# Attention and a feed-forward layer on one core: five units whose softmax weights and values are multiplied whole, as float32

## The chip, the core and the metric

The kernel runs on one core of a Trainium2 chip. The core has a matrix engine (PE, with its weight loads shown as PEld), a vector engine (DVE), an activation engine (ACT), a general engine (POOL, called gpsimd in the code) and a queue that starts transfers (SP). Each takes its instructions in a fixed order, and they wait for one another by semaphores. The metric is the device time of one execution in microseconds (us); lower is better.

## The reference

```python
scores = scale * np.matmul(q, k.transpose(0, 1, 3, 2))          # 8 batches, 8 heads, 576 x 64
thresh = np.max(scores, axis=-1, keepdims=True) - tau           # tau = 0.02
scores = np.where(scores >= thresh, scores, -1000000000.0)
scores = scores - np.max(scores, axis=-1, keepdims=True)
attn = np.exp(scores)
attn = attn / (np.sum(attn, axis=-1, keepdims=True) + 1e-09)
x = np.matmul(attn, v)                                          # heads side by side: 4608 x 512
h = x @ w_in                                                    # 512 -> 2048
g = np.maximum(h, 0.0) + np.log1p(np.exp(-np.abs(h)))
return g @ w_out                                                # 2048 -> 512
```

Inputs of the attention are float32. The two weight matrices arrive in eight bytes a number and are brought to float32 on the chip. A score just above or just below the threshold changes a row of weights wholly, so products are kept near float32 precision.

## The kernel before, in words

**Units and tiles.** A unit is one batch and one pair of heads: 32 units, in the code `s`. Each has nine tiles of 128 query rows: four of the first head, four of the second, and one (index `NC` = 4) that holds the last 64 rows of both. `g` counts tiles over all units, 0 to 287. For a tile the kernel makes scores on PE (`scores`, L410), the negated row maximum on DVE (`row_max`, L416), exponentials on ACT (`exps`, L424), and the masked exponentials with their row sum on DVE (`mask`, L429). PE transposes them (`weights_T`, L463; the 64 rest columns of two tiles at once, L460), ACT copies them to SBUF (`weights_hi`), and when a group of tiles is there, `values` multiplies them with the values, L536 to L538. A unit has four groups `g` of 256 or 320 columns.

**Two halves.** Most products are made from halves in a reduced type (float32r). `x` is split into `hi`, its rounded copy, and `lo`, what is missing. For the weights that is a tile `gH` with five column blocks (four main blocks and one block that holds the rest rows' high half above their low half) and a tile `gL` with the low part of the four main blocks. For the values it is `vt`: 64 columns of high part beside 64 columns of low part, made on POOL by `split_v` (L118 and L125). A group then takes nine matmuls: four of `gH` and four of `gL` with `vt`, and one for the rest block. The two halves of the output partitions are added: ACT copies one half to `xp`, DVE adds the other (`values_out`).

**Two ways to the low part.** For the first four units (`s.neg`, tiles under `TG` = 36) DVE is spared: PE transposes the exponentials a second time into a bank `tl` (L511), subtracts the high part there by a product with the negative `gH` and an identity (L513), and ACT copies the result to `gL`. DVE still makes the low half of the rest block (L523). From the fifth unit on, DVE subtracts straight from the score bank (L125).

**Order.** The program is written out tile by tile from a string of steps: `PAT0` for the first 36 tiles, `PAT` after them. Letters stand for the steps: R row maximum of the next tile, M mask, T transposes, e exponentials of the next tile, S scores two tiles ahead, h and l the high and low parts, x the extras (values, the next unit's splits and transposes), w one piece of weight preparation every second tile (`W1` = 2, 32 pieces in all), p a point at which deferred steps come due, f feed-forward matmuls. A scheduler may shift neighbouring instructions. Feed-forward work comes by quota per tile and starts about tile 36; the first chunk of 512 tokens is due from tile 41. After the last tile the rest of it runs alone.

**Buffers.** There are two score banks, two halves of `e_all`, four PSUM banks `g` shared by everything else, three `nat` buffers (k, q, v as loaded), three `vt` buffers and two each of `gH` and `gL`.

**Weight pieces.** A piece is loaded, then ACT takes an absolute value (L185), POOL clamps it (L186), DVE puts its bits together in three instructions (L192, L194, L197) and POOL splits it (L118, L125). Feed-forward copies and subtractions are recorded at these last lines too, so the tile name tells them apart.

Of the kernel before, what the change touches and what calls it, by code (L numbers as in the profile page):

```python
# [58 lines left out]
def tile_kernel(ctx: ExitStack, tc: tile.TileContext, q, k, v, tau, w_in, w_out, out):  # L59
# [207 lines left out]
    for b in range(B):  # L267
        for kind in (("one", "two") if b < NSPLIT else ("all",)):
            for hp in range(NPAIR):
# [15 lines left out]
                s.neg = 9 * NPAIR * b + 9 * hp < TG  # L285
# [20 lines left out]
    def load_v(s):  # L306
        s.vn = apool.tile([P, 10, D], F32, tag="nat", bufs=3, name=f"vn_{s.i}")
# [173 lines left out]
    def copy(s, out_, in_):  # L481
        if s.neg:
            nc.scalar.activation(out_, in_, AF.Copy, scale=-1.0)
        else:
            nc.scalar.copy(out_, in_)  # L485

    def weights_hi(s, t):
        main, rest = s.sp[t]
        for g, c0, s0, n in s.place[t]:
            copy(s, group(s, g)[0][:, 0:NC, c0:c0 + n], main[:, :, s0:s0 + n])  # L490
        both = rests(s, t)
        if len(both) == 2:

# [8 lines left out]
    def weights_lo(s, t):
        main, rest = s.sp.pop(t)
        for g, c0, s0, n in s.place[t]:
            h, l = group(s, g)
            if s.neg:
                if s0 == 0:
                    low = ps_g.tile([P, NC, P], F32, tag="g", name=f"tl_{s.i}_{t}")
                    for c in range(NC):
# [1 line left out]
                        nc.tensor.matmul(low[:, c, :], e_all[:, s.half[t], k0:k0 + P], ident, is_transpose=True,  # L511
                                         start=c == 0, stop=False)
                nc.tensor.matmul(low[:, :, s0:s0 + n], identr, h[:, 0:NC, c0:c0 + n], start=False, stop=s0 + n == P)  # L513
# [5 lines left out]
        for x, rows, up, down in rests(s, t):
            for g, c0, s0, n in s.place[x]:  # L520
                h = group(s, g)[0]
                if s.neg:
                    nc.vector.scalar_tensor_tensor(out=h[down, NC, c0:c0 + n], in0=rest[rows, s0:s0 + n], scalar=-1.0,  # L523
                                                   in1=h[up, NC, c0:c0 + n].bitcast(F32), op0=ALU.mult, op1=ALU.subtract)
                else:
                    lo_of(nc.vector, h[down, NC, c0:c0 + n], rest[rows, s0:s0 + n], h[up, NC, c0:c0 + n])
# [14 lines left out]
    def values_out(s, g, o):  # L541
# [4 lines left out]
        copy(s, xs, o[move, 0:n])  # L546
        if s.neg:
            nc.vector.tensor_tensor(out=xs, in0=xs, in1=o[keep, 0:n], op=ALU.subtract)
        else:
# [431 lines left out]
```

## Time and profile before

| | |
|---|---|
| median of 3 runs | 1475.11 us (1473.59 to 1477.98) |
| profiled execution | 1474.09 us, span 1472.3 us |
| mean granted PE clock | 0.991 |
| PE busy | 1405.8 us (95%) |
| PEld busy | 1192.3 us (81%) |
| DVE busy | 1013.3 us (69%) |
| ACT busy | 872.2 us (59%) |
| POOL busy | 604.7 us (41%) |

Busy time is the union of an engine's instruction spans. Matmuls are pipelined, so the spans of neighbours overlap: a matmul's price in a full queue is the distance from one start to the next, not its own length. The whole-program shares mix stages: about 140 us of attention alone, a long middle in which attention and feed-forward share PE, and a tail of feed-forward alone.

### The profile page before, as it was taken

The numbers are of one execution on the slowest core, as the hardware profiler recorded it, in microseconds if no ns is written. First come the engines' busy times: TensorE is split into PE (matmuls) and PEld (weight loads), VectorE is DVE, ScalarE is ACT, GpSimd is POOL, SyncE is SP. The second block draws the span as 40 slices with busy tenths as digits, with TensorE's granted clock in tenths as the row PEclk, the third lists the DMA queues.
The fourth block names the chain that finished last, engine by engine and source line by source line (L and its number), as shares of the span: only waits on it lengthen the run. The fifth ranks groups of instructions, "written<-read, shape, count | busy, mean of one in ns | idle before, by whom it ended". The sixth has DMA issues, their size and how long they took to land.

```text
span 1472.3 us, 23929 instructions
## 1 busy us (share of the span) xinstructions
PE 1405.8 (95%) x8024; PEld 1192.3 (81%) x8024; DVE 1013.3 (69%) x2251; ACT 872.2 (59%) x1671; POOL 604.7 (41%) x629
## 2 busy tenths in 40 slices
PE   6878789999999999999999999999999999999998
PEld 5767677788888888888888888888888888788886
DVE  6998778877777777777777777777777777411211
ACT  6887577566766576656666666657665665411110
POOL 3767565544333433343334433343334332323221
PEclk9999899999999999999999999999999999999999
DMA  5777565434344554335334534454433533344321
GB/s 149 213 203 199 168 200 161 134 111 135 109 121 117 129 150 121 110 107 153 108 101 116 140 106 117 117 139 142 119 113 107 159 93 82 101 136 128 116 86 43
DMA packets 131210, 189.95 MB, mean 129 GB/s; under 512 B 35312, under 2 KB 86800, under 8 KB 131088
## 3 DMA queue, kind: packets, MB, share of 16 engines
q1 hardware_dynamic: 131088, 188.43, 44.2%
q8 instruction: 64, 1.05, 0.3%
q14 instruction: 58, 0.48, 0.1%
HBM read 140.51 MB, written 27.41 MB: 114 GB/s over the span
## 4 chain that ended last, share of the span: by engine, by line
PE 74%; DVE 8%; ACT 7%; issue 4%; POOL 3%; DMA 3%; SPq 1%; POOLq 0%; DVEq 0%; ACTq 0%
PE s L410 10%; PE h L631 8%; PE h L629 8%; PE h L633 8%; PE o L691 7%; PE o L689 7%; PE o L687 7%; PE s L463 7%; PE pv L536 3%; PE pv L537 3%; DVE negm L416 2%; PE tr L351 2%; DVE e_all L429 2%; POOL g L125 1%; DMA wc_i<-in_moe_w_in_dram 1%
## 5 line engine op out<-in xcount | busy, mean ns | idle before, releaser
L485 ACT CAST gH<-s 128x512 fp32r<-128x512 f32 (+1 forms) x448 | 186.7, 466 | 160.8 <-PE s L463 152.8
L125 POOL TENSOR_TENSOR g<-st,g 128x512 fp32r<-128x512 f32 x144 | 192.8, 1357 | 194.2 <-DVE g L122 182.3
L429 DVE SCALAR_TENSOR_TENSOR e_all<-s,thr,e_all 128x576 f32<-128x576 f32 x288 | 234.3, 815 | 37.8 <-ACT e_all L424 34.8
L416 DVE TENSOR_REDUCE negm<-s 128x1 f32<-128x576 f32 x288 | 217.4, 755 | 41.4 <-PE s L410 33.4
L691 PE MATMUL o<-wo_o,g 128*128 128x512 f32 x576 | 232.6, 404 | 5.3 <-POOL g L125 5.3
L631 PE MATMUL h<-xl,wi 128*128 128x512 f32 x576 | 233.1, 405 | 1.7 <-POOL xl L125 1.7
L687 PE MATMUL o<-wo_o,g 128*128 128x512 f32 x576 | 232.9, 404 | 1.0 <-ACT st L651 0.7
L629 PE MATMUL h<-xh,wi 128*128 128x512 f32 x576 | 230.6, 401 | 1.9 <-ACT st L651 1.4
L633 PE MATMUL h<-xh,wi 128*128 128x512 f32 x576 | 230.4, 400 | 0.0
L689 PE MATMUL o<-wo_o,g 128*128 128x512 f32 x576 | 229.7, 399 | 0.0
L424 ACT ACTIVATE e_all<-s,negm 128x576 f32<-128x576 f32 x288 | 215.8, 750 | 10.3 <-DVE negm L416 6.5
L125 DVE TENSOR_TENSOR gL<-s,gH 128x512 fp32r<-128x512 f32 (+1 forms) x280 | 175.0, 633 | 59.1 <-ACT gH L485 55.8
L410 PE MATMUL s<-kT,qT 128*128 128x288 f32 x1024 | 194.3, 311 | 13.3 <-DVE gH L125 5.9
L410 PEld LDWEIGHTS s<-kT,qT 128*128 128x128 f32 x1024 | 150.5, 192 | 33.9 <-issue 11.4
L122 DVE CAST g<-st 128x512 fp32r<-128x512 f32 x128 | 57.4, 485 | 149.6 <-ACT st L651 149.1
L463 PE MATMUL s<-identr,e_all 128*128 128x128 f32 x1008 | 155.7, 277 | 3.8 <-DVE e_all L429 3.8
L651 ACT ACTIVATE st<-h 128x512 f32<-128x512 f32 x144 | 78.3, 596 | 117.3 <-PE h L633 116.7
L536 PE MATMUL pv<-gH,vt 128*128 128x320 f32 (+1 forms) x512 | 143.9, 301 | 1.4 <-ACT gH L485 1.3
L537 PE MATMUL pv<-gL,vt 128*128 128x320 f32 (+1 forms) x512 | 142.8, 300 | 1.5 <-DVE gL L125 1.4
L691 PEld LDWEIGHTS o<-wo_o,g 128*128 128x128 f32 x576 | 108.7, 189 | 29.6 <-POOL g L125 11.0
L463 PEld LDWEIGHTS s<-identr,e_all 128*128 128x128 f32 x1008 | 116.2, 142 | 19.2 <-DVE e_all L429 10.9
L629 PEld LDWEIGHTS h<-xh,wi 128*128 128x128 f32 x576 | 108.9, 189 | 25.4 <-ACT st L651 1.9
(105 smaller groups left out, 2381.1 us busy)
## 6 DMA issues: line engine op xcount, KB each, us to landing
wi<-wi_d SPq DMA_DIRECT2D x144, 512.0 KB
qT<-qT SPq DMA_DIRECT2D x124, 128.0 KB
R<-r_d SPq DMA_DIRECT2D x64, 144.0 KB
kn<-in_k_dram SPq DMA_DIRECT2D x32, 256.0 KB
qn<-in_q_dram SPq DMA_DIRECT2D x32, 256.0 KB
vn<-in_v_dram SPq DMA_DIRECT2D x32, 256.0 KB
wc_i<-in_moe_w_in_dram SPq DMA_DIRECT2D x16, 512.0 KB
wi_d<-wc_i SPq DMA_DIRECT2D x32, 256.0 KB
```

What stands on the lines that cost most here:

```text
L125: eng.tensor_tensor(out=out_, in0=in_, in1=hi.bitcast(F32), op=ALU.subtract)
L410: nc.tensor.matmul(sp[:, hf, 0:HS], lhs, s.kT[j][:, k0 + hf * HS:k0 + (hf + 1) * HS], start=(m == 0), stop=(m == len(parts) - 1))
L416: nc.vector.reduce_max(negm, s.sp[t][:, :, 0:HS], axis=AX.XY, negate=True)
L424: nc.scalar.activation(e_all[:, s.half[t], :].rearrange("p (h n) -> p h n", h=2), s.sp[t][:, :, 0:HS], AF.Exp, bias=s.m[t][0], scale=1.0)
L429: masked.append(nc.vector.scalar_tensor_tensor(out=e2, in0=s.sp[t][:, :, 0:HS], scalar=s.m.pop(t)[1], in1=e2, op0=ALU.is_ge, op1=ALU.mult, ...
L463: nc.tensor.matmul(main[:, c, :], e[:, c0:c0 + P], ident, is_transpose=True, start=True, stop=True)
L629: nc.tensor.matmul(h, wi[:, 0, cc, :], u.h[cc], start=(cc == 0), stop=False)
L631: nc.tensor.matmul(h, wi[:, 0, cc, :], u.l[cc], start=False, stop=False)
L633: nc.tensor.matmul(h, wi[:, 1, cc, :], u.h[cc], start=False, stop=(cc == NCC - 1))
L687: nc.tensor.matmul(o, gh[:, sl], wo[fc][:, 0, :], start=(i == 0), stop=False)
L689: nc.tensor.matmul(o, gh[:, sl], wo[fc][:, 1, :], start=False, stop=False)
L691: nc.tensor.matmul(o, gl[:, sl], wo[fc][:, 0, :], start=False, stop=(i == QF - 1))
```

## The change

For the first five units (`s.whole`, `NF` = 5: the four pairs of batch 0 and the first pair of batch 1) the weights stay whole float32 in `gH`, `gL` is not made, the values are used as they were loaded, and the product is a plain float32 matmul. `split_v` returns at once for them. The loaded values take a `vt` buffer in place of a `nat` buffer. The output has 64 partitions, and ACT copies it to `xp`; no addition follows. The rest block of a group now holds rest rows in one half and zeros in the other: where one rest tile serves two tiles, two ACT instructions write it with a scale per partition of 1 or 0 (`side`, filled once at the start); in the tile of the last 64 rows ACT copies and POOL writes the zeros. The path with the negative copies is gone altogether, so units 0 to 3 lose L511, L513 and L523, and unit 4 loses its subtractions on DVE.

```diff
+    side = cpool.tile([P, 2], F32, name="side")
+    for i in range(2):
+        for j in range(2):
+            nc.vector.memset(side[i * SR:(i + 1) * SR, j:j + 1], float(i == j))
...
-                s.neg = 9 * NPAIR * b + 9 * hp < TG
+                s.whole = len(units) < NF
...
     def load_v(s):
-        s.vn = apool.tile([P, 10, D], F32, tag="nat", bufs=3, name=f"vn_{s.i}")
+        if s.whole:
+            s.vn = apool.tile([P, 10, D], F32, tag="vt", bufs=3, name=f"vn_{s.i}")
+        else:
+            s.vn = apool.tile([P, 10, D], F32, tag="nat", bufs=3, name=f"vn_{s.i}")
...
     def split_v(s, j):
+        if s.whole:
+            return
...
         for g, c0, s0, n in s.place[t]:
-            copy(s, group(s, g)[0][:, 0:NC, c0:c0 + n], main[:, :, s0:s0 + n])
+            h = group(s, g)[0]
+            h = h.bitcast(F32) if s.whole else h
+            nc.scalar.copy(h[:, 0:NC, c0:c0 + n], main[:, :, s0:s0 + n])
...
+                elif len(both) == 2:
+                    nc.scalar.activation(h.bitcast(F32), rest, AF.Copy, scale=side[:, s.half[x]:s.half[x] + 1])
+                else:
+                    nc.scalar.copy(h[up].bitcast(F32), rest[rows, s0:s0 + n])
+                    nc.gpsimd.memset(h[down].bitcast(F32), 0.0)
 
     def weights_lo(s, t):
         main, rest = s.sp.pop(t)
+        if s.whole:
+            return
...
-                    for c in range(NC):
-                        k0 = s.half[t] * SR + c * P
-                        nc.tensor.matmul(low[:, c, :], e_all[:, s.half[t], k0:k0 + P], ident, is_transpose=True,
-                                         start=c == 0, stop=False)
-                nc.tensor.matmul(low[:, :, s0:s0 + n], identr, h[:, 0:NC, c0:c0 + n], start=False, stop=s0 + n == P)
...
     def values(s, g):
...
+        if s.whole:
+            for c in range(NC + 1):
+                nc.tensor.matmul(o[0:D, 0:n], s.vn[:, 5 * j + c, :], h[:, c, 0:n].bitcast(F32),
+                                 start=(c == 0), stop=(c == NC))
+            defer(1, lambda: nc.scalar.copy(s.xp[j * D:(j + 1) * D, x0:x0 + n], o[0:D, 0:n]))
+            return
```

On PE, the end of unit 0's last group (`pv_3`) and the second tile of unit 1, before. A row gives line, operation, output<-inputs and shape; `tr` and `tm` are the transposed rest and main blocks, `s` a score bank, `tl` the bank for the low part, `rT` the transposed row scales.

```order
L536 MATMUL pv_3_663<-gH_3_556,vt_1_230 128x256
L537 MATMUL pv_3_663<-gL_3_557,vt_1_230 128x256
L538 MATMUL pv_3_663<-gH_3_556,vt_1_230 128x256
L460 MATMUL tr_1_685<-identr,e_all 128x128
L463 MATMUL tm_1_684<-identr,e_all 128x128 x4
L410 MATMUL s_137<-kT_0_377,qT_1_0_427 128x288 x2
L410 MATMUL s_137<-kT_0_377,qT_1_0_428 128x288 x2
L511 MATMUL tl_1_698<-identr,e_all 128x128 x4
L513 MATMUL tl_1_698<-gH_0_651,identr 128x512
L560 MATMUL rT_709<-identr,rs_614 9x128
```

The same place after (the new kernel's own lines: its L538 is the float32 product).

```order
L538 MATMUL pv_3_560<-gH_3_482,vn_183 64x256 x5
L472 MATMUL tr_1_577<-identr,e_all 128x128
L475 MATMUL tm_1_576<-identr,e_all 128x128 x4
L422 MATMUL s_142<-kT_0_339,qT_1_0_379 128x288 x2
L422 MATMUL s_142<-kT_0_339,qT_1_0_380 128x288 x2
L565 MATMUL rT_593<-identr,rs_519 9x128
```

The nine products of the group are five, the tile's second set of transposes and the subtraction are gone, and what stands around them keeps its order.

On DVE, from the end of unit 0 into unit 1's second tile, before: `negm` is a row maximum, `e_all,sums` a mask, `wa_i` a weight piece, `gH` the low half of a rest block, `xp` the addition of the two output halves.

```order
L548 TENSOR_TENSOR xp_327<-xp_327,pv_2_568 64x320
L556 RECIPROCAL rs_614<-rs_614 128x9
L429 SCALAR_TENSOR_TENSOR e_all,sums_551<-s_138,thr_0_585,e_all 128x576
L523 SCALAR_TENSOR_TENSOR gH_3_556<-tr_8_590,gH_3_556 64x128 x2
L416 TENSOR_REDUCE negm_1_636<-s_137 128x1
L194 SCALAR_TENSOR_TENSOR wa_i_3_579<-wc_i_3_578,wa_i_3_579 128x512
L416 TENSOR_REDUCE negm_2_679<-s_138 128x1
L429 SCALAR_TENSOR_TENSOR e_all,sums_551<-s_137,thr_1_637,e_all 128x576
L197 SCALAR_TENSOR_TENSOR wa_i_3_579<-wc_i_3_578,wa_i_3_579 128x512
L548 TENSOR_TENSOR xp_327<-xp_327,pv_3_663 64x256
```

And after.

```order
L561 RECIPROCAL rs_519<-rs_519 128x9
L441 SCALAR_TENSOR_TENSOR e_all,sums_477<-s_143,thr_0_498,e_all 128x576
L428 TENSOR_REDUCE negm_1_541<-s_142 128x1
L201 SCALAR_TENSOR_TENSOR wa_i_3_493<-wc_i_3_492,wa_i_3_493 128x512
L428 TENSOR_REDUCE negm_2_571<-s_143 128x1
L441 SCALAR_TENSOR_TENSOR e_all,sums_477<-s_142,thr_1_542,e_all 128x576
L204 SCALAR_TENSOR_TENSOR wa_i_3_493<-wc_i_3_492,wa_i_3_493 128x512
```

The rest blocks and the additions have left the queue; maxima, masks and weight pieces stand in the same order.

On PE in unit 4, from the scores of the tile with the last 64 rows (`qm`) on, before: `pv_1` is the second group, `h_0` and `h_1` are feed-forward products.

```order
L410 MATMUL s_137<-kT_1_1837,qm 128x288 x4
L351 MATMUL tr_0_1_2162<-identr,q_5_0_2084 128x128 x3
L460 MATMUL s_138<-identr,e_all 128x128
L463 MATMUL s_138<-identr,e_all 128x128 x4
L351 MATMUL tr_0_1_2162<-identr,q_5_0_2084 128x128
L410 MATMUL s_138<-kT_1_1837,qT_4_1_1843 128x288 x2
L410 MATMUL s_138<-kT_1_1837,qT_4_1_1844 128x288 x2
L463 MATMUL s_137<-identr,e_all 128x128 x4
L466 MATMUL s_137<-identr,e_all 64x128
L536 MATMUL pv_1_2209<-gH_1_2030,vt_0_1740 128x320
```

And after.

```order
L472 MATMUL s_143<-identr,e_all 128x128
L475 MATMUL s_143<-identr,e_all 128x128 x4
L363 MATMUL tr_0_1_1749<-identr,q_5_0_1674 128x128 x4
L634 MATMUL h_0_1739<-xh_0_1715,wi_0_1733 128x512
L636 MATMUL h_0_1739<-xl_0_1716,wi_0_1733 128x512
L638 MATMUL h_0_1739<-xh_0_1715,wi_0_1733 128x512
L634 MATMUL h_0_1739<-xh_2_1725,wi_0_1733 128x512
L422 MATMUL s_143<-kT_1_1466,qT_4_1_1472 128x288 x2
L422 MATMUL s_143<-kT_1_1466,qT_4_1_1473 128x288 x2
```

Between the transposes into a score bank and the scores that reuse it there now stand four transposes of the next unit's queries and four feed-forward matmuls, where one such transpose stood.

More of the change, by code (lines that the diff above doesn't have):

```diff
@@ L51 @@
 GV = 1
+NF = 5
 TG = 36
@@ L435, in group @@
             h = apool.tile([P, NC + 1, 320], F32R, tag="gH", name=f"gH_{s.i}_{g}")
-            l = apool.tile([P, NC, 320], F32R, tag="gL", name=f"gL_{s.i}_{g}")
+            l = None if s.whole else apool.tile([P, NC, 320], F32R, tag="gL", name=f"gL_{s.i}_{g}")
             s.grp[g] = (h, l)
@@ L489, in weights_hi @@
         for g, c0, s0, n in s.place[t]:
-            copy(s, group(s, g)[0][:, 0:NC, c0:c0 + n], main[:, :, s0:s0 + n])
+            h = group(s, g)[0]
+            h = h.bitcast(F32) if s.whole else h
+            nc.scalar.copy(h[:, 0:NC, c0:c0 + n], main[:, :, s0:s0 + n])
         both = rests(s, t)
-        if len(both) == 2:
+        if len(both) == 2 and not s.whole:
             (g, c0, _, n), = s.place[both[0][0]]
-            copy(s, group(s, g)[0][:, NC, c0:c0 + 2 * n].rearrange("p (k n) -> p k n", k=2),
-                 rest.unsqueeze(1).to_broadcast([P, 2, n]))
+            nc.scalar.copy(group(s, g)[0][:, NC, c0:c0 + 2 * n].rearrange("p (k n) -> p k n", k=2),
+                           rest.unsqueeze(1).to_broadcast([P, 2, n]))
@@ L497, in weights_hi @@
             return
-        for x, rows, up, _ in both:
+        for x, rows, up, down in both:
             for g, c0, s0, n in s.place[x]:
-                copy(s, group(s, g)[0][up, NC, c0:c0 + n], rest[rows, s0:s0 + n])
+                h = group(s, g)[0][:, NC, c0:c0 + n]
+                if not s.whole:
+                    nc.scalar.copy(h[up], rest[rows, s0:s0 + n])
+                elif len(both) == 2:
[3 more added lines that the diff above has]
+                    nc.gpsimd.memset(h[down].bitcast(F32), 0.0)
@@ L516, in weights_lo @@
-        if s.neg:
-            defer(1, lambda: [copy(s, group(s, g)[1][:, :, c0:c0 + n], low[:, :, s0:s0 + n])
-                              for g, c0, s0, n in s.place[t]])
+            lo_of(nc.vector, l[:, :, c0:c0 + n], main[:, :, s0:s0 + n], h[:, 0:NC, c0:c0 + n])
         for x, rows, up, down in rests(s, t):
@@ L521, in weights_lo @@
                 h = group(s, g)[0]
[L522 to L526, printed above, removed]
+                lo_of(nc.vector, h[down, NC, c0:c0 + n], rest[rows, s0:s0 + n], h[up, NC, c0:c0 + n])
     def values(s, g):
@@ L532, in values @@
         h, l = s.grp[g]
+        o = ps_g.tile([P, 512], F32, tag="g", name=f"pv_{s.i}_{g}")
+        if s.whole:
[4 more added lines that the diff above has]
+            return
         vt = s.vt[j]
-        o = ps_g.tile([P, 512], F32, tag="g", name=f"pv_{s.i}_{g}")
         for c in range(NC):
@@ L545, in values_out @@
         xs = s.xp[keep, x0:x0 + n]
[L546 to L549, printed above, removed]
-            nc.vector.tensor_tensor(out=xs, in0=o[keep, 0:n], in1=xs, op=ALU.add)
+        nc.scalar.copy(xs, o[move, 0:n])
+        nc.vector.tensor_tensor(out=xs, in0=o[keep, 0:n], in1=xs, op=ALU.add)
     def row_scales(s):
```

10 lines of the change are left out of this document (removed).

## The prediction

> **What bounds the kernel now.** I read the busy time by unit first: the stretches are unit 0, units 1 to 3, unit 4 (bounds taken from each unit's first mask on DVE), and one late stretch. The columns are length, then busy us of PE, PEld, DVE, ACT and POOL, the granted PE clock, and the DMA share.
>
> ```profile
> 15.50:44.70 29.20, 24.74 (x172) 22.63 (x172) 22.79 (x49) 23.00 (x55) 14.34 (x20) 1.00 0.56 163
> 44.70:74.50 29.80, 26.14 (x187) 22.24 (x184) 28.31 (x56) 26.05 (x62) 20.76 (x22) 1.00 0.78 215
> 74.50:108.50 34.00, 25.75 (x187) 22.30 (x185) 30.67 (x60) 28.65 (x68) 22.86 (x25) 1.00 0.71 207
> 108.50:140.70 32.20, 27.24 (x182) 24.80 (x182) 29.07 (x57) 23.99 (x57) 21.78 (x26) 0.89 0.68 187
> 140.70:189.60 48.90, 39.41 (x208) 32.15 (x207) 37.58 (x79) 31.70 (x60) 32.19 (x35) 0.86 0.63 189
> ...
> 600.00:1300.00 700.00, 692.31 (x4035) 591.68 (x4034) 509.00 (x1171) 437.33 (x810) 259.27 (x264) 1.00 0.42 120
> ```
>
> Late in the program PE is the bound (692.31 of 700 us). In units 1 to 3 it is not: over their 96.0 us DVE is busy 88.05 us (91.7%), PE 79.13 (82.4%), ACT 78.69. The waits of that stretch (total us, times, longest) say the same: PE's two largest are for the mask on DVE.
>
> ```profile
> PE tm L463 <- DVE e_all L429: 6.8, 4, 2.9
> PE tr L460 <- DVE e_all L429: 6.3, 5, 2.5
> ...
> ACT wa_i L185 <- DMA wc_i<-in_moe_w_in_dram: 2.3, 3, 1.1
> ```
>
> The feed-forward quota is counted per tile. Whatever shortens the first 45 tiles moves everything after them forward, and nothing later hands it back unless the work per tile grows.
>
> **DVE in units 0 to 3.** The groups of DVE instructions in the same 96.0 us show what goes.
>
> ```profile
> L429 DVE SCALAR_TENSOR_TENSOR e_all<-s,thr,e_all 128x576 f32<-128x576 f32 x28 | 22.6, 809 | 1.2 <-ACT e_all L424 1.0
> L416 DVE TENSOR_REDUCE negm<-s 128x1 f32<-128x576 f32 x27 | 20.3, 753 | 1.7 <-PE s L410 1.4
> L523 DVE SCALAR_TENSOR_TENSOR gH<-tr,gH 64x128 fp32r<-64x128 f32 x24 | 6.9, 289 | 0.5
> ...
> L548 DVE TENSOR_TENSOR xp<-xp,pv 64x320 f32<-64x320 f32 x6 | 2.9, 484 | 0.5 <-ACT xp L483 0.4
> L548 DVE TENSOR_TENSOR xp<-xp,pv 64x256 f32<-64x256 f32 x6 | 2.5, 417 | 1.7 <-ACT xp L483 1.7
> ...
> L523 DVE SCALAR_TENSOR_TENSOR gH<-tr,gH 64x64 fp32r<-64x64 f32 x6 | 1.0, 213 | 0.1
> ```
>
> Maxima and masks stay. L523 and L548 leave: 6.9 + 1.0 + 2.9 + 2.5 = 13.3 us in three units, 4.4 a unit. DVE falls from 29.35 to 24.9 us a unit.
>
> **PE in units 0 to 3.** Prices are distances from start to start. The columns are start, length, engine, line.
>
> ```profile
> 25.98 0.28 PE L536 MATMUL pv<-gH,vt 128*128 128x256 f32 x1
> ...
> 27.05 0.27 PE L460 MATMUL tr<-identr,e_all 128*128 128x128 f32 x1
> ...
> 42.67 0.31 PE L537 MATMUL pv<-gL,vt 128*128 128x320 f32 x1
> ...
> 43.26 0.27 PE L460 MATMUL tr<-identr,e_all 128*128 128x128 f32 x1
> ...
> 54.54 0.60 PE L511 MATMUL tl<-identr,e_all 128*128 128x128 f32 x4
> 54.90 0.48 PE L513 MATMUL tl<-gH,identr 128*128 128x512 f32 x1
> 55.21 0.28 PE L536 MATMUL pv<-gH,vt 128*128 128x256 f32 x1
> ```
>
> Nine products of 256 columns take 27.05 - 25.98 = 1.07 us, 0.119 each; four of 320 columns take 0.59 us, 0.1475 each. Two groups of either width cost 2 x 1.07 + 18 x 0.1475 = 4.80 us a unit, and these go. The low part costs 0.36 us for four transposes and 0.31 us for the subtraction: 9 x 0.67 = 6.03 us a unit, which go too.
>
> What comes is 20 plain float32 matmuls a unit, and no row shows one. The lower end is one pass at the reduced type's price: 10 x 0.119 + 10 x 0.1475 = 2.67 us. For the upper end I use what this kernel does itself: a number that the reduced type can't hold is two halves, and the whole product of two such numbers has four terms (the feed-forward part writes three and drops low times low). Four passes at the same rows' price are 10.66 us. I take four: a plain float32 matmul has no reason to drop a term. The weight loads I take as hidden, as today's are: a load lasts 0.188 us (rows below) and the products behind each other still start 0.119 us apart.
>
> [...]
>
> PE a unit is then 10.66 - 4.80 - 6.03 = -0.2 us: 26.4 becomes 26.2. PE gains nothing; its work changes kind.
>
> **ACT, POOL, buffers.**
>
> ```profile
> L483 ACT ACTIVATE gL<-tl 128x512 fp32r<-128x512 f32 x24 | 14.4, 600 | 5.3 <-PE tl L513 5.2
> ...
> L483 ACT ACTIVATE gH<-tr 128x256 fp32r<-128x256 f32 x12 | 4.6, 386 | 0.0
> ...
> L483 ACT ACTIVATE gL<-tl 128x256 fp32r<-128x256 f32 x6 | 2.0, 378 | 0.4 <-PE tl L513 0.3
> ...
> L383 ACT ACTIVATE qm<-tr,qscale 128x64 fp32r<-128x64 f32 x6 | 1.6, 327 | 0.0
> ```
>
> ACT loses (14.4 + 2.0) / 3 = 5.5 us a unit of `gL` copies. Four rest copies of 0.386 become eight with a scale per partition; between 0.327 (L383, half as wide) and 0.386 (twice as wide), say 0.35: +1.3 us. Net -4.2 us, 26.2 to 22.0 a unit. POOL loses the split of the values and gets two small memsets a unit. They stand behind the weight pieces in POOL's order, and the products of two groups wait for them:
>
> ```profile
> POOL wa_i L186 <- ACT wa_i L185: 14.2, 8, 4.0
> ```
>
> That clamp has waited up to 4.0 us. The group's products are written a tile (3.5 us) after the memset, so I take nothing, up to 0.5 us a memset. The memsets of `side` stand at the start, where DVE waits for the first loads. The values' loads keep their number and place on SP; only their buffer changes, to one free since three units before. Nothing for both.
>
> **The pace of units 0 to 3.** The longest engine is now PE with 26.2 us a unit. I give it the share that DVE, the longest today, reaches: 26.2 / 0.917 = 28.6 us against 32.0, -3.4 a unit, -10.2 for three. In unit 0 PE is already the longest: (24.74 - 0.2) / 0.917 = 26.8 against 29.2, -2.4. Together -12.6 us.
>
> **Unit 4.** Here nothing is saved on PE: +10.66 - 4.80 = +5.9 us, while feed-forward matmuls fill its queue. DVE loses its subtractions:
>
> ```profile
> L125 DVE TENSOR_TENSOR gL<-s,gH 128x512 fp32r<-128x512 f32 x8 | 5.5, 683 | 5.6 <-ACT gH L485 5.6
> ...
> L125 DVE TENSOR_TENSOR gH<-s,gH 64x128 fp32r<-64x128 f32 x8 | 2.3, 288 | 0.2
> ...
> PE s L410 <- DVE gH L125: 3.5, 1, 3.5
> ...
> PE pv L537 <- DVE gL L125: 0.8, 1, 0.8
> ...
> 158.23 1.30 PE L410 MATMUL s<-kT,qT 128*128 128x288 f32 x4 [3.53 <-DVE gH L125]
> ...
> 161.49 0.63 PE L629 MATMUL h<-xh,wi 128*128 128x512 f32 x1
> 161.92 0.63 PE L631 MATMUL h<-xl,wi 128*128 128x512 f32 x1
> ...
> 166.09 0.40 PE L633 MATMUL h<-xh,wi 128*128 128x512 f32 x1
> 166.32 0.39 PE L629 MATMUL h<-xh,wi 128*128 128x512 f32 x1
> ```
>
> Scores wait for the bank until DVE's last subtraction has read it: 3.5 us once. That wait goes with its cause, and so does the 0.8. Behind the long gap PE runs slowly: the same matmul starts every 0.43 us at 161.5 and every 0.23 us at 166. Some 5 us run so, of which 5 x (1 - 0.23/0.43) = 2.3 come back. Unit 4: +5.9 - 4.3 - 2.3 = -0.7 us.
>
> **The sum** is -12.6 - 0.7 = -13.3 us: span 1472.3 to 1459.0, this execution 1474.09 to 1460.8. The median shown is 1.0 above this execution, so **1462 us**.
>
> **Rivals.** *DVE stays the bound and PE fits under it.* For it: DVE holds the longest waits today. Units 1 to 3 go to 24.9 / 0.917 = 27.2 us, -4.8 each; with unit 0 and 4 as above -17.5: 1458. Against it: PE has more work than DVE.
>
> *The weight pieces take the cover's place.* A piece is loaded a fixed number of steps, about one tile, ahead of its ACT instruction, and ACT has waited 2.3 us for such loads. Tiles that are 3.4 / 9 = 0.38 us shorter give each of the 18 pieces in 36 tiles that much less lead: up to 6.8 us back, in ACT's queue ahead of the exponentials. Net -6.5: 1469. Against it: only three such waits in 27 tiles.
>
> *Slower: the float32 loads stand in the open.* A load today:
>
> ```profile
> L536 PEld LDWEIGHTS pv<-gH,vt x48: 187/188/333, 47.2 to 138.6; 128*128 128x128 f32 x48
> ```
>
> With 64 columns, half of 0.188 us, before each of 80 passes: +7.5 us a unit. PE has 33.7 us, at 0.917 36.8 a unit: +4.8 in three, (24.5 + 7.5) / 0.917 = 34.9 in unit 0, +5.7, and 7.5 - 0.7 in unit 4: +27: 1502. It turns slower once PE passes 32.0 x 0.917 = 29.3 us a unit, 0.04 us a pass. Against it: every load of the trace hides behind the product before it. Any dearer pass than assumed acts at this place.
>
> *Float32 at one pass*, so that the products aren't what the change says: 2.67 us a unit, DVE bound, unit 4 at -2.1 - 4.3 - 2.3 = -8.7: -25.5, 1450. For it: four float32 transposes (L511) cost only 0.09 us each. Against it: a transpose multiplies with ones and zeros.
>
> **How the numbers follow.** Forecast 0.48, DVE bound 0.15, weight pieces 0.18, slower 0.13, one pass 0.05; 0.01 for no effect. The range 1451 to 1475 leaves out the slower case and the one pass. A difference under 0.3% (4.4 us) can't be told from no change. The forecast, the DVE case and the one pass are faster, the weight pieces in three of four, so faster 0.79, within 0.3% 0.08, slower 0.13.
>
> **What would show it.** Right: each float32 product of 320 columns takes about 0.59 us start to start, of 256 about 0.48; a unit of batch 0 takes 28 to 29 us; DVE is under 90% busy there and PE over it; the 3.5 us wait in unit 4 is gone; from 190 us on, all is as before and 13 us earlier. Wrong: products over 0.75 us (five passes); longer waits of ACT's L185 for loads; PE waiting for `gH` behind a POOL memset; or a later stage that takes longer than now.

## The result, and the profile after

| | before | after |
|---|---|---|
| median, same chip | 1474.35 us (1472.26 to 1477.98, 4 runs) | 1458.26 us (1457.67 to 1461.06, 4 runs) |
| profiled execution: span | 1472.3 us | 1456.1 us |
| mean granted PE clock | 0.991 | 0.996 |
| PE / DVE / ACT / POOL busy | 1405.8 / 1013.3 / 872.2 / 604.7 us | 1398.7 / 983.5 / 854.7 / 588.5 us |

The ratio is 0.9893 [0.9875, 0.9911]: 16.1 us less by the medians, 16.2 by the spans. The forecast was 1462 us and 13.3 us less. The size was about right; the place was not.

The next rows give the kernel after by stage: unit 0, units 1 to 3, unit 4. The columns are those of the prediction's first fence: length, then busy us of PE, PEld, DVE, ACT and POOL, the granted PE clock, the DMA share. Units begin at their first mask on DVE.

```profile
14.99:44.70 29.71, 24.05 (x130) 18.33 (x130) 19.65 (x38) 19.88 (x49) 10.62 (x16) 1.00 0.64 189
44.70:136.85 92.15, 75.17 (x423) 52.46 (x423) 71.43 (x129) 65.91 (x168) 57.59 (x70) 0.94 0.72 203
136.85:176.07 39.22, 36.19 (x187) 24.18 (x188) 26.52 (x53) 27.80 (x59) 26.34 (x31) 1.00 0.70 214
```

Units 0 to 3 went from 125.2 us to 121.9, and unit 4 from 49.0 to 39.2. From the start of unit 4 to the start of unit 8 the time fell from 173.9 to 162.2 us. From there to the end it is 1157.7 and 1157.1 us.

Each float32 product leaves two records (x10 for five). The timeline of PE shows a group of five products of 256 columns, and one of 320, each with what starts next:

```profile
24.90 2.54 PE L538 MATMUL pv<-gH,vn 128*64 128x256 f32 x10
27.37 0.33 PE L472 MATMUL tr<-identr,e_all 128*128 128x128 f32 x1
...
33.58 2.90 PE L538 MATMUL pv<-gH,vn 128*64 128x320 f32 x10
36.41 0.33 PE L472 MATMUL tr<-identr,e_all 128*128 128x128 f32 x1
```

Five products take 27.37 - 24.90 = 2.47 us and 36.41 - 33.58 = 2.83 us, start to start: 0.49 and 0.57 us a product.

The waits of units 0 to 3 after (total us, times, longest):

```profile
PE tm L475 <- DVE e_all L441: 23.1, 17, 3.3
...
DVE e_all L441 <- ACT e_all L436: 16.4, 14, 2.7
...
ACT xp L540 <- PE pv L538: 12.4, 10, 3.4
POOL gH L516 <- PE pv L538: 9.1, 5, 4.2
...
ACT wa_i L192 <- DMA wc_i<-in_moe_w_in_dram: 7.0, 3, 3.5
```

PE waits for the mask on DVE (L441), the mask for the exponentials on ACT (L436), and ACT's copy of the output (L540) for the product. It is a ring in which everybody waits, and in units 1 to 3 nobody is busy more than 75.17 of 92.15 us (PE, 82%).

In unit 4 the feed-forward matmuls are the clearest difference. First before, then after (busy us, mean ns of one):

```profile
L629 PE MATMUL h<-xh,wi 128*128 128x512 f32 x20 | 9.2, 470 | 1.4 <-ACT st L651 1.4
L633 PE MATMUL h<-xh,wi 128*128 128x512 f32 x19 | 8.5, 449 | 0.0
L631 PE MATMUL h<-xl,wi 128*128 128x512 f32 x19 | 8.3, 439 | 1.7 <-POOL xl L125 1.7
```

```profile
L634 PE MATMUL h<-xh,wi 128*128 128x512 f32 x16 | 6.7, 418 | 0.0
...
L636 PE MATMUL h<-xl,wi 128*128 128x512 f32 x15 | 6.2, 413 | 0.4 <-POOL xl L132 0.4
L638 PE MATMUL h<-xh,wi 128*128 128x512 f32 x15 | 6.1, 406 | 0.0
```

Twelve fewer fall into unit 4 (46 for 58), which at 0.23 us from start to start (the prediction's rows at 166.09 and 166.32) is 2.8 of the 9.8 us. They come later: counted to the start of unit 8 each trace has 310 of them.

### The profile page after: what moved, and what is told of

It is laid out like the page before. It is cut to its first block, busy times and chain, and to the rows that moved or that the text cites. A ratio compares the mean times of both kernels' runs of the same rounds, so it can differ in the third digit from the quotient of the medians.

```text
span 1456.1 us, 23475 instructions
## 1 busy us (share of the span) xinstructions
PE 1398.7 (96%) x7860; PEld 1162.6 (80%) x7860; DVE 983.5 (68%) x2175; ACT 854.7 (59%) x1651; POOL 588.5 (40%) x619
## 4 chain that ended last, share of the span: by engine, by line
PE 77%; DVE 7%; ACT 5%; issue 3%; POOL 3%; DMA 3%; SPq 1%; POOLq 0%; ACTq 0%; DVEq 0%
PE s L422 10%; PE h L636 8%; PE h L634 8%; PE h L638 8%; PE o L696 8%; PE o L694 7%; PE o L692 7%; PE s L475 7%; PE pv L544 3%; PE pv L545 3%; PE pv L538 2%; PE tr L363 2%; DVE e_all L441 2%; DVE negm L428 1%; ACT L656 1%
## 5 line engine op out<-in xcount | busy, mean ns | idle before, releaser
L441 DVE SCALAR_TENSOR_TENSOR e_all<-s,thr,e_all 128x576 f32<-128x576 f32 x288 | 234.4, 815 | 55.1 <-ACT e_all L436 51.8
L499 ACT CAST gH<-s 128x512 fp32r<-128x512 f32 (+1 forms) x270 | 144.8, 549 | 141.6 <-PE s L475 139.9
L436 ACT ACTIVATE e_all<-s,negm 128x576 f32<-128x576 f32 x288 | 215.7, 749 | 10.6 <-DVE negm L428 6.5
L132 DVE TENSOR_TENSOR gL<-s,gH 128x512 fp32r<-128x512 f32 (+1 forms) x270 | 168.9, 634 | 49.0 <-ACT gH L499 23.6
L422 PEld LDWEIGHTS s<-kT,qT 128*128 128x128 f32 x1024 | 149.1, 191 | 28.7 <-issue 13.3
L696 PEld LDWEIGHTS o<-wo_o,g 128*128 128x128 f32 x576 | 108.4, 188 | 29.0 <-POOL g L132 10.9
L634 PEld LDWEIGHTS h<-xh,wi 128*128 128x128 f32 x576 | 108.3, 188 | 23.0 <-ACT xh L127 0.4
L692 PEld LDWEIGHTS o<-wo_o,g 128*128 128x128 f32 x576 | 108.5, 188 | 22.1 <-DVE g L129 1.9
L638 PEld LDWEIGHTS h<-xh,wi 128*128 128x128 f32 x576 | 108.4, 188 | 21.5
```

Of the source, the lines that this page charges most:

```text
L132: eng.tensor_tensor(out=out_, in0=in_, in1=hi.bitcast(F32), op=ALU.subtract)
L422: nc.tensor.matmul(sp[:, hf, 0:HS], lhs, s.kT[j][:, k0 + hf * HS:k0 + (hf + 1) * HS], start=(m == 0), stop=(m == len(parts) - 1))
L436: nc.scalar.activation(e_all[:, s.half[t], :].rearrange("p (h n) -> p h n", h=2), s.sp[t][:, :, 0:HS], AF.Exp, bias=s.m[t][0], scale=1.0)
L441: masked.append(nc.vector.scalar_tensor_tensor(out=e2, in0=s.sp[t][:, :, 0:HS], scalar=s.m.pop(t)[1], in1=e2, op0=ALU.is_ge, op1=ALU.mult, ...
L634: nc.tensor.matmul(h, wi[:, 0, cc, :], u.h[cc], start=(cc == 0), stop=False)
L638: nc.tensor.matmul(h, wi[:, 1, cc, :], u.h[cc], start=False, stop=(cc == NCC - 1))
```

## The experiments

Every run was timed beside the kernel before. Lengths of stretches are from one profiled execution each. To the start of unit 8 such an execution agrees with the difference of the medians only within about 4 us, so verdicts go by the medians.

| run | median us | ratio to before | units 0 to 3, us | unit 4, us | its PE clock | units 4 to 7, us |
|---|---|---|---|---|---|---|
| before | | 1 | 125.2 | 49.0 | 0.86 | 173.9 |
| the change | 1458.26 | 0.9893 [0.9875, 0.9911] | 121.9 | 39.2 | 1.00 | 162.2 |
| four units whole | 1464.69 | 0.9954 [0.9941, 0.9966] | 123.0 | 46.2 | 0.89 | 168.3 |
| only unit 4 whole | 1466.54 | 0.9967 [0.9952, 0.9981] | 126.0 | 40.2 | 1.00 | 165.7 |
| output copy later | 1459.53 | 0.9915 [0.9893, 0.9936] | 120.9 | 39.4 | 0.96 | 165.0 |
| DVE copies put back | 1467.82 | 0.9981 [0.9963, 0.9999] | 130.8 | 43.5 | 0.92 | 166.2 |
| one pass | 1467.22 | 0.9967 [0.9954, 0.9980] | 120.3 | 47.1 | 0.78 | 169.2 |
| products in two parts | 1460.47 | 0.9923 [0.9908, 0.9937] | 121.4 | 43.3 | 0.96 | 169.8 |
| DVE copy in each tile | 1464.03 | 0.9944 [0.9923, 0.9964] | 125.5 | 39.7 | 0.96 | 164.8 |
| DVE reads the bank in unit 4 | 1455.69 | 0.9891 [0.9873, 0.9908] | 121.2 | 38.5 | 1.00 | 159.5 |
| one pass, four times | 1458.31 | 0.9906 [0.9892, 0.9921] | 120.5 | 43.4 | 0.92 | 163.4 |
| longer lead | 1453.48 | 0.9872 [0.9853, 0.9891] | 116.0 | 37.1 | 1.00 | 168.0 |
| no bit steps | 1451.93 | 0.9863 [0.9849, 0.9878] | 111.9 | 42.3 | 0.96 | 166.6 |
| six units whole | 1457.70 | 0.9893 [0.9867, 0.9918] | 124.3 | 37.8 | 1.00 | 162.9 |

### Which units the time came from

Two runs do one part of the change alone. The first leaves unit 4 as before:

```diff
-NF = 5
+NF = 4
```

> Only units 0 to 3 keep whole weights; unit 4 goes back to high and low parts, with DVE's subtractions. By the prediction's own split (-12.6 us from units 0 to 3, -0.7 from unit 4) nearly all of the gain stays: 1459 to 1461 us against 1474.4. By the masks of the two traces (units 0 to 3 end 3.8 us earlier, the start of unit 7 15.6 us earlier) units 0 to 3 give 3 to 5 us and unit 4 the rest: 1468 to 1472 us.

The second is the kernel before with unit 4 alone whole:

```diff
+                s.whole = len(units) == 4
```

> The kernel before, with whole weights in unit 4 alone (its subtractions on DVE and its value split on POOL gone, five float32 products a group). By the prediction -0.7 us: 1473 to 1475. By the traces' masks -10 to -12 us: 1462 to 1465, with units 0 to 3 ending at about 140.7 us as before and unit 7 starting some 11 us earlier.

Units 0 to 3 alone are worth 0.46% (6.8 us against the 1471.46 us of the same chip), unit 4 alone 0.33% (4.9 us). Together they give 11.7 us, somewhat less than the 16.1 of the change, whose interval starts at 13 us. Unit 4 in the two runs, by stretch:

```profile
137.94:184.13 46.19, 38.78 (x206) 31.24 (x206) 35.27 (x76) 30.99 (x60) 32.02 (x35) 0.89 0.65 199
```

```profile
141.57:181.79 40.22, 35.17 (x189) 24.17 (x187) 25.97 (x54) 28.59 (x59) 28.89 (x32) 1.00 0.70 209
```

Unit 4 is short where it is whole, also with the units ahead of it as before, and long and slow where it isn't: over all runs of the table it takes 37.1 to 43.5 us at a clock of 0.92 to 1.00 with float32 products, and 46.2 and 49.0 us at 0.89 and 0.86 without the change in it. So the two parts of the prediction's sum are both real, but the first (-12.6) is about half as large and the second (-0.7) many times larger.

### Units 0 to 3: what sets the pace

**Is it ACT's copy of the output?** It waits 12.4 us for the product in front of other ACT work. Here it stands one point later and behind the exponentials:

```diff
-            defer(1, lambda: nc.scalar.copy(s.xp[j * D:(j + 1) * D, x0:x0 + n], o[0:D, 0:n]))
+            defer(2, lambda: behind(nc.scalar.copy(s.xp[j * D:(j + 1) * D, x0:x0 + n], o[0:D, 0:n]), expd))
```

> The changed kernel, but ACT copies a float32 product to xp one point later and behind the next tile's exponentials, so these no longer stand behind a copy that waits for the 2.4 to 2.85 us product on PE. Theory 'copy in the way' (the changed trace has 12.4 us of ACT waits for that product in units 0 to 3): units 0 to 3 together take 109 to 116 us in place of 121.9, the time is 1448 to 1454. Rival 'PE itself' (the products are one block on PE and the next tile's transposes stand behind them, whatever ACT does): units 0 to 3 take 120 to 122 us, the time is 1457 to 1459.

Units 0 to 3 take 120.9 us and the median is 1459.53: no difference. The wait moved. Rows of the waits of units 0 to 3:

```profile
ACT e_all L436 <- PE tr L472: 15.5, 13, 2.2
...
PE tm L475 <- DVE e_all L441: 9.7, 5, 3.3
```

PE's wait for the mask fell from 23.1 to 9.7 us, and ACT's exponentials now wait 15.5 us for PE. What was taken from one place of the ring came up at the next.

**Is it the length of the block of products?** Five products in a row keep PE from the next transposes for up to 2.83 us. Here three are issued, and two behind the next scores:

```diff
-            for c in range(NC + 1):
...
+            if s.i < 4:
+                some(range(NSP))
+                defer(2, rest_of)
+                return
```

> The changed kernel, but in units 0 to 3 each group's five float32 products are issued as three, and two more behind the next tile's transposes and scores. PE does the same work; the longest block goes from 2.85 to 1.7 us. Theory 'PE block': units 0 to 3 take 112 to 118 us in place of 121.9, time 1450 to 1456. Rival 'PE load as a whole, or a wait elsewhere': 120 to 123 us, 1457 to 1460.

Units 0 to 3 take 121.4 us and the median is 1460.47 us, no better than the change: no.

**Is it PE's work at all?** Here the five units' weights and values are rounded to float32r and multiplied once (the run with one pass), with no low parts; the values go through `nat` and POOL rounds them, as before the change.

```diff
-                nc.tensor.matmul(o[0:D, 0:n], s.vn[:, 5 * j + c, :], h[:, c, 0:n].bitcast(F32),
+                nc.tensor.matmul(o[0:D, 0:n], s.vt[j][:, c, 0:D], h[:, c, 0:n],
```

> The changed kernel, but the whole units' weights and values are only rounded to the reduced type and multiplied in one pass, with no low parts (so their low parts are left out of the result; POOL makes the rounded values, 0.5 us a group of columns). Only the price of the products on PE falls, from about 2.4 and 2.85 us a group to about 0.6 and 0.75. Theory 'PE block' (the long products hold up the next tile's transposes and what follows): units 0 to 3 together take 108 to 114 us in place of 121.9. Rival 'something else sets the pace' (weight pieces, loads, the chain of mask, transposes and exponentials): 119 to 122 us. In unit 4 about 8 us less PE work. Time 1438 to 1448 by the first, 1448 to 1453 by the second.

Units 1 to 3, and the largest wait of units 0 to 3:

```profile
41.94:136.51 94.57, 59.96 (x369) 54.11 (x369) 68.31 (x127) 65.08 (x164) 54.56 (x70) 0.80 0.66 187
```

```profile
PE tm L471 <- DVE e_all L437: 30.6, 14, 4.5
```

PE has 15 us less to do in units 1 to 3 (59.96 for 75.17) and they take 94.57 us for 92.15. So the amount of PE's work does not set the pace there by itself. The comparison is not clean, though. The granted clock is 0.80 for 0.94, so what PE still does is probably slower (shown for unit 4 alone: identical transposes took 341 ns there at 0.78, and 279 in the change at 1.00), and these units hold one wait of scores for a transfer of queries that the change doesn't have:

```profile
PE s L418 <- DMA qT<-qT: 4.6, 1, 4.6
```

The median, 1467.22 us, lies above both expected ranges. The rival that products of one pass would save 25.5 us falls too, since even with one pass the kernel is slower than the change by 0.9967 - 0.9893 = 0.7%, about 11 us. In the profiles 7.9 us of that arise in unit 4, below.

**Is it DVE?** Three runs alter DVE's work. The first puts DVE's copies of the rest blocks and of the outputs back into units 0 to 3:

```diff
+            for x, rows, up, down in rests(s, t) if s.i < 4 else []:
+                for g, c0, s0, n in s.place[x]:
+                    nc.vector.tensor_scalar(out=group(s, g)[1][down, 0, 0:n], in0=rest[rows, s0:s0 + n],
+                                            scalar1=1.0, scalar2=None, op0=ALU.mult)
...
+        nc.scalar.copy(xs, o)
+        if s.i < 4:
+            nc.vector.tensor_scalar(out=l[0:D, 1, 0:n], in0=o, scalar1=1.0, scalar2=None, op0=ALU.mult)
```

> The changed kernel with as many DVE instructions put back in units 0 to 3 as the change took away (rest blocks and output halves copied from PSUM to a tile that nobody reads, about 4 us a unit). If DVE still sets the pace of units 0 to 3, these take 4 us each longer: 136 to 139 us in place of 121.9 and a time of 1472 to 1475. If DVE now has slack and PE with ACT sets the pace, under 1.5 us a unit: 122 to 128 us, 1458 to 1464.

Units 0 to 3 take 130.8 us, more than before the change and between the two expected ranges. But this run mixes two causes, as its waits of units 0 to 3 show:

```profile
DVE gL L558 <- ACT xp L556: 15.0, 6, 3.6
```

DVE's new copy waits for the product and then for ACT, and the masks queue behind it. That is a wait put into the ring, not work alone. The second run adds work that waits for nothing new, a copy of 384 columns a tile straight behind the transposes:

```diff
+            if s.i < 4:
+                nc.vector.tensor_scalar(out=group(s, s.place[t][0][0])[1], in0=main[:, 0:3, :], scalar1=1.0, scalar2=None,
+                                        op0=ALU.mult)
```

> The changed kernel with one DVE copy of 384 columns from the transposed weights per tile in units 0 to 3 (to a tile that nobody reads): about 0.5 us a tile, 4.3 us a unit, as much as the change took away, but no instruction that waits for the float32 products. If DVE still sets the pace: units 0 to 3 take 135 to 139 us, the time is 1471 to 1475. If DVE has slack: 122 to 128 us, 1458 to 1464.

The third takes work away, the three bit steps of each weight piece in about the first 36 tiles, so that these weights are left unassembled:

```diff
         def second(n):
-            if n == 0:
+            i = None
+            if now["p"] < 78:
+                pass
+            elif n == 0:
```

> The change without the three bit steps that DVE does for each weight piece in the first 36 tiles, so that the lower parts of those weights are left as they were in their buffers: what is left out is the splitting of these weights, about 11 us of DVE a unit. Theory that DVE's pieces stand in the loop and so set the pace (a mask waits behind them, and TensorE's next transposes behind the mask): units 0 to 3 take 105 to 113 us (122 in the change) and the time falls by 9 to 16 us, to 1442 to 1449. Rival, that DVE is no longer what the loop waits for: 118 to 122 us, time 1454 to 1459.

Units 1 to 3 of the two, first with the added work, then without the bit steps:

```profile
45.73:140.36 94.63, 75.45 (x426) 53.58 (x426) 81.70 (x158) 67.42 (x170) 60.48 (x71) 0.95 0.72 208
```

```profile
44.70:127.11 82.41, 69.97 (x424) 49.80 (x423) 44.49 (x90) 66.47 (x168) 50.01 (x65) 1.00 0.74 221
```

Beside the change (92.15 us with 71.43 us of DVE) 10.3 us more of DVE make these units 2.5 us longer, and 26.9 us less make them 9.7 us shorter. Part of the 2.5 us is scatter. Two runs below have the code of the change in units 1 to 3, the one in which DVE reads the bank in unit 4 and the one with six units whole, and they took:

```profile
43.04:136.45 93.41, 74.61 (x423) 52.96 (x423) 72.02 (x129) 66.46 (x168) 59.12 (x70) 0.95 0.70 202
```

```profile
45.75:139.20 93.45, 76.13 (x423) 53.82 (x423) 72.19 (x129) 66.51 (x168) 58.34 (x70) 0.93 0.70 202
```

Against these three executions the added work costs 1.2 to 2.5 us and the removed work saves 9.7 to 11.0: between 0.12 and 0.40 us for each us of DVE. The step from before to after lies in that range (DVE 88.05 to 71.43, length 96.0 to 92.15, which is 0.23), though it changes ACT's and PE's work too. By the medians the added work is clear of noise: 0.9944 for 0.9893, about 7.5 us, of which the profiles have 3.6 in units 0 to 3. That DVE alone still sets the pace falls: 125.5 us where 135 to 139 were expected. I read this as a ring in which a DVE instruction counts where a mask stands behind it; no run tries that reading by itself. The theory that DVE's pieces stand in the ring holds for units 0 to 3 (111.9 us, expected 105 to 113). The whole kernel gained less than that theory gave: 1451.93 us, where 1442 to 1449 were expected.

**Is it the loads of the weight pieces?** Here a piece's first compute step stands two points later behind its load. In these tiles that is one tile; the expectation says two.

```diff
-WD = 2
+WD = 4
```

> The change with one number altered, WD 2 to 4: the first compute step of a weight piece stands two tiles further behind its load. Theory that the waits of ACT for the weight pieces' loads (9.8 us in units 0 to 3 of the change) set the pace there: they fall under 3 us, units 0 to 3 take 112 to 117 us (122 in the change) and the time is 1449 to 1454. Rival, that the loop from the mask by the transposes and exponentials to the next mask sets it: ACT waits elsewhere instead, 120 to 122 us, time 1456 to 1460.

The time came out as that theory had it: 116.0 us in units 0 to 3, and 1453.48 us. Its reason did not. ACT's waits for such loads in units 0 to 3: in the kernel before, in the change (its first row is shown above), and here:

```profile
ACT wa_i L185 <- DMA wc_i<-in_moe_w_in_dram: 5.0, 4, 2.7
```

```profile
ACT wa_o L192 <- DMA wc_o<-in_moe_w_out_dram: 2.8, 3, 1.4
```

```profile
ACT wa_i L192 <- DMA wc_i<-in_moe_w_in_dram: 9.2, 6, 3.5
ACT wa_o L192 <- DMA wc_o<-in_moe_w_out_dram: 0.6, 1, 0.6
```

7.0 + 2.8 us in the change, 9.2 + 0.6 here: the same 9.8 us. So the longer lead helps, but not by shorter load waits; perhaps it puts the pieces' steps at a better place between the masks. What it does is left open.

### Unit 4: what became faster

**Is it the subtraction that DVE no longer makes?** In the prediction's wait of 3.5 us scores waited for DVE's last read of the bank, a subtraction of a rest block (`gH`). Here DVE subtracts the main blocks (`gL`) from the bank in unit 4 again, and the result is not used; the rest blocks' subtractions (2.3 us in the prediction's row) stay out.

```diff
+            for g, c0, s0, n in s.place[t] if s.i == 4 else []:
+                h, l = group(s, g)
+                nc.vector.tensor_tensor(out=l[:, :, c0:c0 + n], in0=main[:, :, s0:s0 + n],
+                                        in1=h[:, 0:NC, c0:c0 + n].bitcast(F32), op=ALU.subtract)
```

> The changed kernel with DVE's subtraction from the score bank put back in unit 4 alone (its result is read by nobody): 6.3 us of DVE work, and each score bank is free only after it. If unit 4's gain came from this chain (transposes, copy, subtraction, next scores), unit 4 takes 43 to 48 us in place of 39.2 and the time is 1461 to 1466. If it came from elsewhere (POOL's splits, the rest blocks, the products), unit 4 takes 39 to 41 us, 1457 to 1460.

Unit 4, the subtraction's row, and PE's wait for it:

```profile
136.41:174.93 38.52, 34.24 (x178) 23.24 (x178) 31.27 (x62) 28.55 (x60) 28.25 (x31) 1.00 0.71 214
```

```profile
L525 DVE TENSOR_TENSOR gL<-s,gH 128x512 f32<-128x512 f32 x8 | 5.5, 685 | 3.7 <-ACT gH L515 2.0 <-ACT gH L501 1.6
```

```profile
PE s L422 <- DVE gL L525: 1.2, 3, 0.8
```

The main blocks' subtractions are back with their 5.5 us, yet PE waits for them only 1.2 us in all, never longer than 0.8. Unit 4 stays at 38.5 us and the ratio, 0.9891, is that of the change. So these subtractions were not the cause of the gain. The rest blocks' subtractions, at which the long wait ended, are not tried alone. But in the run with one pass unit 4 has no subtraction of either kind, and it takes 47.1 us: to be rid of them is not enough for a short unit.

**Is it that dearer products keep PE busy?** In the run with one pass unit 4 took 47.1 us. Rows of its stretch, then two groups of identical instructions in it, transposes (L471) and scores (L418):

```profile
136.50:183.65 47.15, 33.47 (x163) 25.79 (x163) 25.84 (x55) 27.65 (x56) 31.91 (x36) 0.78 0.65 200
```

```profile
L418 PE MATMUL s<-kT,qT 128*128 128x288 f32 x32 | 8.2, 392 | 5.1 <-ACT gH L508 3.0 <-ACT gH L510 1.5 <-ACT gH L494 0.7
L471 PE MATMUL s<-identr,e_all 128*128 128x128 f32 x36 | 7.7, 341 | 5.0 <-DVE e_all L437 5.0
```

PE's two largest waits in the same unit:

```profile
PE s L471 <- DVE e_all L437: 5.0, 4, 1.7
PE s L418 <- ACT gH L508: 3.0, 2, 1.8
```

The next run is that kernel with each one-pass product issued four times. Values, buffers and POOL's work are as in the run with one pass; PE is given work that changes no result.

```diff
-            for c in range(NC + 1):
+            for c in 4 * list(range(NC + 1)):
```

> The kernel of the one-pass run (products of the five units on values rounded to float32r, one pass, no lower parts, values by way of the buffer nat, rounded on POOL), with one edit: each of its products is issued four times, so that TensorE works on them about as long as on the float32 products of the change, while the values take the same way and POOL does the same work as in the one-pass run. Theory that a TensorE kept busy holds its granted clock: unit 4 takes 39 to 42 us at a mean clock of 0.97 to 1.00 (47.2 at 0.78 in the one-pass run) and the time is 1456 to 1462. Rival, that the way of the values (nat, the roundings on POOL) makes unit 4 slow: it stays at 45 to 48 us and the time is 1464 to 1469.

```profile
136.60:180.00 43.40, 37.20 (x225) 30.80 (x225) 25.45 (x50) 28.02 (x60) 28.08 (x32) 0.92 0.63 189
```

```profile
L418 PE MATMUL s<-kT,qT 128*128 128x288 f32 x32 | 6.3, 323 | 0.1
L471 PE MATMUL s<-identr,e_all 128*128 128x128 f32 x36 | 5.5, 276 | 1.0 <-DVE e_all L437 1.0
```

```profile
PE h L629 <- ACT xh L127: 3.4, 1, 3.4
```

Issuing every product four times makes the kernel faster, from 1467.22 to 1458.31 us, and as fast as the change; the intervals of the two ratios lie well apart. The rival that the way of the values makes unit 4 slow falls. Identical transposes take 276 ns in place of 341, identical scores 323 in place of 392, and the granted clock is 0.92 for 0.78. Unit 4 itself missed the expected 39 to 42 us by 1.4 and the expected clock of 0.97 to 1.00: it holds a wait of 3.4 us for feed-forward input. PE stood idle for 47.15 - 33.47 = 13.7 us in the one case and for 6.2 in the other. The extra products went into time in which PE had stood idle, so they cost little; that the time fell on top of that goes with the higher clock. It is one pair of kernels, and the placement of the feed-forward matmuls differs by four in unit 4 (48 and 44), so the share of the clock in the 8.9 us is not measured by itself. For units 4 to 7 the two runs take 169.2 and 163.4 us, and kernels with one and the same code there spread as widely (below). That the busier PE and its clock are the cause is the likeliest reading, not a proof.

In these rows the clock is lower where PE stood idle longer: 0.78 with 13.7 us idle in unit 4, 0.92 with 6.2, 1.00 with 3.0 in the change. Idle time alone does not fix it: in the prediction's rows before the change, PE in unit 2 stood idle 8.3 of 34.0 us at 1.00 and in unit 3 5.0 of 32.2 at 0.89. Nor does a single long gap stand behind the 0.78: no wait of unit 4 in the run with one pass is longer than 1.8 us, and units 1 to 3 ahead of it ran at 0.80 already, with waits of up to 4.6 us. What sets the clock is not shown.

**And the next unit?** If the fifth unit paid since PE was idle and slow in unit 4, the sixth, which runs at clock 1.00 anyway, should give nothing:

```diff
-NF = 5
+NF = 6
```

> The change with one number altered, NF 5 to 6: the next pair of batch 1 (unit 5) is whole too. In the change unit 5 already runs at a granted clock of 1.00, so nothing is to be won there by keeping TensorE busy. Theory that the fifth unit paid because TensorE was idle and slowed in unit 4: here the dearer products only add PE time (about 5.9 us by the prediction's working), less the subtractions that DVE loses; by the start of unit 8 the kernel is 2 to 6 us behind the change (301 to 305 us against 299.0) and the time is 1458 to 1463. Rival, that a whole unit is cheaper beside the feed-forward products as such: another gain of the fifth unit's size, 1450 to 1454, unit 8 starting at 291 to 295 us.

Unit 5, in this run and in the change:

```profile
176.98:220.40 43.42, 41.77 (x217) 29.97 (x216) 26.07 (x52) 31.23 (x62) 27.66 (x32) 1.00 0.66 193
```

```profile
176.07:215.62 39.55, 38.24 (x218) 30.41 (x217) 32.37 (x72) 30.11 (x56) 27.80 (x29) 1.00 0.71 207
```

DVE is spared 6.3 us in the unit, PE is busy 3.5 us longer, and the unit takes 3.9 us more. Unit 8 starts at 302.1 us for 299.0, inside the expected 301 to 305, but that is luck: 2.5 of the 3.1 us arise in units 0 to 3, whose code is the change's (124.3 for 121.9 us), and units 4 to 7 take 162.9 for 162.2. The median, 1457.7 us, is 0.3 below the expected range and the ratio is that of the change. A gain of the fifth unit's size is ruled out.

### What is handed back

The kernels that run the change's own code from unit 4 on take 162.2 (the change), 165.0, 166.2, 169.8 and 164.8 us there (output copy later, DVE copies put back, products in two parts, DVE copy in each tile), and 166.6 us without the bit steps. The run without bit steps won 10.0 us in units 0 to 3 and lost 4.4 in units 4 to 7. The same code thus takes up to 7.6 us more or less there, I take it by the state in which the first 36 tiles leave the queues and by the scatter of single executions; no run separates the two. What the change does to unit 4 is more than that for unit 4 by itself (49.0 and 46.2 us as before; 37.1 to 43.5 us in the ten kernels that have float32 products there). For units 4 to 7 as a whole it isn't clearly more: 168.3 us with unit 4 as before lies inside the spread, and 173.9 outside.

## Why the prediction was right or wrong

**The float32 product: right.** Forecast 0.48 and 0.59 us, measured 0.49 and 0.57, so 2 x 2.47 + 2 x 2.83 = 10.6 us a unit for 10.66. The four passes were an estimate from the four terms of a product of two halves; no run shows passes as such. What the trace shows is the price: 0.57 us is 3.8 times the 0.1475 us of the reduced type's product, and 0.49 is 4.2 times 0.119. The price spoke against the change, and it was foreseen rightly; it lay in time that PE had (9.5 us idle in unit 4 before, 3.0 after).

**DVE, ACT and PE in units 1 to 3: right.** Forecast 24.9, 22.0 and 26.2 us a unit; measured 71.43, 65.91 and 75.17 us in three, so 23.8, 22.0 and 25.1. The copies with a scale, the product's weight loads and the masks in three units:

```profile
L441 DVE SCALAR_TENSOR_TENSOR e_all<-s,thr,e_all 128x576 f32<-128x576 f32 x28 | 22.7, 812 | 12.2 <-ACT e_all L436 11.9
...
L538 PEld LDWEIGHTS pv<-gH,vn 128*64 128x64 f32 x120 | 16.7, 148 | 14.1 <-issue 4.4 <-ACT thr L430 0.6 <-ACT qT L376 0.5
...
L513 ACT ACTIVATE gH<-tr,side 128x128 f32<-128x128 f32 x25 | 8.0, 375 | 0.0
```

The scaled copy takes 0.375 us where I had put 0.35. There are two loads a product, 40 a unit, where the slower rival counted 80. Two products of 256 columns start 0.49 us apart with two loads of 0.148 us to each, 0.30 us in all, so the loads lie behind the products and the slower rival did not come.

**The pace of units 0 to 3: wrong, and this is the step that failed.** "I give it the share that DVE, the longest today, reaches: 26.2 / 0.917 = 28.6 us." PE reached 75.17 / 92.15 = 0.82 and a unit takes 30.7 us. In all -3.3 us in the profile where -12.6 was forecast (-6.8 by the medians with four units whole). A share of 0.917 that one engine reaches is no constant that the next engine inherits. The stretch is a ring of waits, in which a us of DVE that was added or taken away was worth 0.12 to 0.40 us. By that the 16.6 us that DVE lost in units 1 to 3 are worth 2 to 7 us, and 3.8 came. That PE gains nothing was nearly right (26.4 to 25.1 us a unit), and mattered little: with 15 us less of PE these units got no shorter, though at a lower clock and with one foreign wait.

**Unit 4: the sign was right, two of its terms were too small.** Forecast +5.9 for the products, -4.3 for waits, -2.3 for the slow clock. Measured with the twelve moved feed-forward matmuls taken off: -9.8 + 2.8 = -7.0 us. PE's idle time went from 48.90 - 39.41 = 9.5 us to 39.22 - 36.19 = 3.0, so -6.5 for waits. With +5.9 for the products that leaves -6.4 for the clock, worked out as a remainder: 0.86 of full speed over the unit, not only for the 5 us behind the one long gap. An estimate from the clock alone, 0.14 of 39.41 us, is 5.5. And the cause I named, DVE's subtraction, does not carry the gain: the main blocks' subtractions put back cost nothing, and without any subtraction the unit took 47.1 us with one pass.

**The rivals.** That DVE stays the bound gave 1458 us, the very time that was measured, but by the wrong way: DVE fell to 71.43 of 92.15 us (78%). The weight pieces were to take back 6.8 us in ACT's waits for loads; in units 0 to 3 these went from 5.0 us to 9.8. That they set the pace is not shown, since the longer lead saved time with the waits unchanged. POOL's memset waits 9.1 us for products, up to 4.2 at a time, where I had taken nothing; what it costs was not tried alone. Two sums of the prediction do not come out: by its own shares the chances are 0.815 for faster and 0.055 for within 0.3%, not 0.79 and 0.08, and the one-pass rival keeps unit 0's -2.4 us, which was worked out with four passes.

**What would show it.** The 3.5 us wait is gone; DVE is under 90%; but PE isn't over 90%, a unit doesn't take 28 to 29 us, and the kernel, 13.6 us ahead at the start of unit 5, is 15.6 ahead from unit 7 on. The forecast of 1462 us came out near 1458 because, in the profiles, an overestimate of 9 us in units 0 to 3 met an underestimate of 11 us in units 4 to 7 (-11.7 for -0.7). That the total came so close was luck.

## What to carry to other kernels

When the longest engine of a stretch is relieved, look first whether the engines wait for one another in a ring; if so, don't hand its busy share to the next engine, but measure the slope: add a known piece of work to one engine and see what part of it the stretch takes, and take the scatter first (three executions of the same code here differed by 1.3 us, half of the smaller effect). Dearer matmuls (2.83 us for 1.33 in a group of 320 columns) came out better than free here, in a unit where PE had gaps and its granted clock was below 1.00: it went from 49.0 us at 0.86 to 39.2 at 1.00. So read the clock and the mean of an unchanged instruction by stretch before adding up prices. And where one engine's wait is removed, put the removed work back without its use, the very instruction at which the wait ended, to see whether it was the cause.

## What the runs showed that I had not expected

Issuing each product of five units four times made the kernel 8.9 us faster. The same transposes took 341 ns at a granted clock of 0.78 and 276 ns at 0.92. A longer lead of the weight pieces (`WD` = 4) on top of the change gives 1453.48 us, 0.9872 [0.9853, 0.9891] of the kernel before, the fastest version here that does the whole work; its interval still touches that of the change. And identical code from unit 4 on took between 162.2 and 169.8 us to the start of unit 8.
